# Counting matmuls of a routing search on four column quarters of the TensorE array

## The chip, the cores and the metric

The kernel runs on 1 core of one Trainium2 chip. The metric is device time in microseconds (us) of one execution, as the median of the runs shown. The profile is one further execution of the same program, with its own time.

## The reference, cut to what matters

Three layers follow each other: a retention attention (8 batches, 8 heads, 576 positions, head size 64), a mixture of 8 experts of which every token uses one, and a dense two-layer block. What the change touches is how tokens are given to experts:

```python
logits = x @ w_gate                      # x: 4608 tokens x 512, 8 experts
order = np.argsort(-logits.flatten())
for idx in order:                        # greedy: the highest logits first
    tok, e = idx // E, idx % E
    if assigned[tok] >= 0 or counts[e] >= cap:      # cap = N // E = 576
        continue
    assigned[tok] = e
    counts[e] += 1
for e in range(E):
    out[assigned == e] = np.maximum(x[assigned == e] @ w1[e], 0) @ w2[e]
...
h = x @ w_in                             # 4608 x 512 @ 512 x 2048
return (np.maximum(h, 0) + alpha * np.minimum(h, 0)) @ w_out
```

## The kernel before

**Stages.** First the attention is worked through in 36 chunks of 128 tokens; it leaves the rows in DRAM and the logits `Lg` (128 partitions x 36 chunks x 8 experts) on chip. Then a loop over `k` from 0 to 7 takes one expert at a time: `expert(k, ...)` runs that expert's two layers on its 576 tokens (matmul lines L913 and L932 to L934), and `second(...)` runs the dense block on 512 of them (first layer L969 to L971, second layer L960 and L991). A last call of `second` does the 64 tokens that are left of each expert. The f32 numbers are split in a high and a low part, so every product takes three matmuls.

**The routing.** `route(k)` finds which expert fills up k-th and which tokens are its own. `route(0)` runs by itself between attention and the first expert. `route(k + 1)` for the others is a generator that runs beside the work on expert `k`: at each call of `tick()` inside `expert` and `second` it writes its next few instructions into the same queues and stops at its next `yield`. A tick in `expert` or the first layer of `second` stands after 12 or 24 matmuls. Nothing reorders the queues afterwards: what stands in an engine's queue runs in that order. Routings 1 to 6 are the same; routing 7 only takes what is left.

**A search in six steps.** A routing looks for the value at which some expert is full. It tries 64, 32, 32, 32, 32 and 65 thresholds in its six steps (`STEPS`). In each step:

- VectorE compares the keys with all thresholds, into `G` (128 x 36 chunks x thresholds, bf16), in two halves of 18 chunks (`compare`, L427).
- One or two ticks later TensorE counts: for each chunk, the 8 columns of `O` (which token has which expert as its best) are the stationary operand and the chunk's part of `G` streams through. The counts add up in a PSUM tile `misc`, 8 rows (experts) by thresholds. Steps 0 and 5 use `counts` (L433): 36 matmuls of 64 or 65 columns with 8 columns of weights, all on the same columns of the array. Steps 1 to 4 use `counts2` (L438): 18 matmuls, each for two chunks, 64 columns long with 40 columns of weights (`O2` holds one chunk's 8 columns at 0 and the next chunk's at 32).
- At the next tick VectorE compares the counts with the room that each expert has (`ind`). After `counts2` it first subtracts the second chunk's counts from the room (`left`, L518) and compares with the first's (L519); after `counts` one instruction (L521) does it.
- At the tick after that TensorE spreads `ind` over 128 partitions (L524), and at the next VectorE adds it up (`sj`, L528), from which the next step's thresholds follow.

`O2` is filled by two ScalarE copies (L457) in the tick in which VectorE has made `O` (L399 to L403). The next tick makes the keys (L405 to L412), the one after it the first comparison.

**What stands around it in the queues.** In `expert`, each matmul tile is taken out of PSUM by ScalarE (L918) and then VectorE (L919, which also reads what L918 wrote). In `second`, VectorE (L974, L976), ScalarE (L978) and VectorE (L979) make `hl` from the first layer's tile. Weights that are new are split by ScalarE (L798) and VectorE (L799); the dense block's weights are split once, during expert 0, and read back split afterwards.

Of the kernel before, what the change touches and what calls it, by code (L numbers as in the profile page):

```python
# [10 lines left out]
F32 = mybir.dt.float32  # L11
F32R = mybir.dt.float32r
BF = mybir.dt.bfloat16
# [4 lines left out]
AF = mybir.ActivationFunctionType  # L18
OP = mybir.AluOpType
# [5 lines left out]
NCH = 36  # L25
# [70 lines left out]
def fused_kernel(ctx: ExitStack, tc: tile.TileContext, att: bass.AP, tab: bass.AP, wg: bass.AP,  # L96
                 w12: bass.AP, w34: bass.AP, alpha: bass.AP, out: bass.AP):
    nc = tc.nc
    V, P, ACT, PE = nc.vector, nc.gpsimd, nc.scalar, nc.tensor
# [3 lines left out]
    keep = ctx.enter_context(tc.tile_pool(name="keep", bufs=1))  # L103
    rt = ctx.enter_context(tc.tile_pool(name="route", bufs=1))
    pr = ctx.enter_context(tc.tile_pool(name="pr", bufs=1, space=bass.MemoryType.PSUM))
# [233 lines left out]


    O = keep.tile([128, NCH, 8], BF, name="O")
    O2 = keep.tile([128, NCH // 2, 40], BF, name="O2")
    vm = keep.tile([128, NCH], F32, name="vm")
    hf = keep.tile([128, NCH], F32, name="hf")
    lf = keep.tile([128, NCH], F32, name="lf")
# [2 lines left out]
    R8 = keep.tile([8, 1], F32, name="R8")  # L348
# [8 lines left out]
    def route_consts():  # L357
        V.tensor_copy(RT[:, 36:38], CONST["pcol"])
        C2["j01"] = CONST["j01"].rearrange("p (z j) -> p z j", z=2)
        V.memset(O2, 0.0)  # L360
        V.memset(Aw, 0.0)
        V.memset(tsum, 0.0)
        V.memset(R8, float(CAP))
        V.memset(ones8, 1.0)
        V.memset(ones8f, 1.0)
        V.tensor_copy(tri, CONST["tri"])
        V.tensor_copy(trii, CONST["trii"])
# [20 lines left out]
    def jt(s):  # L388
        return CONST["jtab"][:, JOFF[s]:JOFF[s + 1]]
# [31 lines left out]
    GT = {}  # L421
# [10 lines left out]
        for c in range(a, b):  # L432
            PE.matmul(GT["p"][0:8, :w], O[:, c, :], GT["G"][:, c, :w], start=c == 0, stop=c == NCH - 1)  # L433

    def counts2(w):

        for i in range(NCH // 2):
            PE.matmul(GT["p"][0:40, :2 * w].rearrange("p (a b) -> p a b", a=2), O2[:, i, :],  # L438
                      GT["G"][:, 2 * i:2 * i + 2, :w], start=i == 0, stop=i == NCH // 2 - 1)

    EXP, IDX, GI = {}, {}, {}

    def route(k):

        ecol, wcol = CONST["ecol"], CONST["wcol"]
        if k == 7:
            m = small("m")
            V.tensor_reduce(m, Lg, axis=AX.X, op=OP.max)
            t8 = small("t8", 1)
            V.tensor_scalar(t8, tsum, -1.0, 36.0, op0=OP.mult, op1=OP.add)  # L450
        else:
            if k:
                best, high, low = prep(0, NCH)
                emit(best)
                Oz = O.rearrange("p (i z) e -> p z i e", z=2)
                for z in range(2):
                    ACT.activation(O2[:, :, 32 * z:32 * z + 8], Oz[:, z], AF.Copy)  # L457
                yield
                emit(high, low)
                yield  # L460
            key, thr, n = hf, jt(0), None
            u = []
            for s, (z, w) in enumerate(STEPS):
                if s == 3:

                    Hb = small("Hb", 1)
                    V.scalar_tensor_tensor(Hb, n, 1.0, u[1], op0=OP.mult, op1=OP.add)
                    key = small("key")
                    V.tensor_scalar(key, hf, Hb, 131072.0, op0=OP.subtract, op1=OP.mult)
                    V.tensor_tensor(key, key, lf, op=OP.add)  # L470
                    thr = jt(3)
                elif s:
                    th = small("thr", 65)
                    V.scalar_tensor_tensor(th[:, :w], n.to_broadcast([128, w]), float(STEPS[s - 1][0]), tb,
                                           op0=OP.mult, op1=OP.add)
                    thr = th[:, :w]
                if k or s:
                    cuts = CUTS if not k else (0, 18, 36)
                    for a, b in zip(cuts, cuts[1:]):
                        compare(key, thr, w, a, b)  # L480
                    if k:
                        yield
                        if s == 5:
                            yield
                    if k and w == 32:
                        counts2(w)
                    else:
                        for a, b in zip(cuts, cuts[1:]):
                            counts(w, a, b)
                else:  # L490
                    best, high, low = prep(33, 36)
                    best.pop(0)()
                    emit(high, best)
                    compare(key, thr, w, 33, 36)
                    emit(low)
                    counts(w, 33, 36)

                if s in (1, 4):
                    tbt = small("tb", 65)
                    V.scalar_tensor_tensor(tbt[:, :STEPS[s + 1][1]], n.to_broadcast([128, STEPS[s + 1][1]]),  # L500
                                           float(STEPS[s - 1][0]), jt(s + 1), op0=OP.mult, op1=OP.add)
                    tb = tbt[:, :STEPS[s + 1][1]]
                    ua = small("ua", 1)
                    zz = STEPS[s - 1][0] + STEPS[s][0] + STEPS[s + 1][0]
                    V.tensor_scalar(ua, n, float(STEPS[s - 1][0]), float((-32768 if s == 1 else 0) - zz),
                                    op0=OP.mult, op1=OP.add)
                elif s in (0, 3):
                    tb = jt(s + 1)
                else:
                    ub = small("ub", 1)  # L510
                    V.scalar_tensor_tensor(ub, n, float(STEPS[s - 1][0]), ua, op0=OP.mult, op1=OP.add)
                    u = [ua, ub]
                yield
                p = GT["p"]
                ind = rt.tile([8, 65], BF, name="ind")
                if k and w == 32:
                    left = rt.tile([8, 32], F32, name="left")
                    V.tensor_scalar(left, p[32:40, w:2 * w], -1.0, R8[:, 0:1], op0=OP.mult, op1=OP.add)  # L518
                    V.tensor_tensor(ind[:, :w], p[0:8, :w], left, op=OP.is_ge)  # L519
                else:  # L520
                    V.tensor_scalar(ind[:, :w], p[0:8, :w], R8[:, 0:1], None, op0=OP.is_ge)  # L521
                if k:
                    yield
                PE.matmul(p[:, 128:128 + w], ones8, ind[:, :w], start=True, stop=True)  # L524
                yield
                sj = small("sj", 65)
                n = small("n", 1, bufs=2)
                V.tensor_scalar(sj[:, :w], p[:, 128:128 + w], 0.5, 0.0, op0=OP.is_ge, op1=OP.add, accum_out=n)  # L528

            j01 = C2["j01"]  # L530
            s8 = rt.tile([8, 2], F32, name="s8")
            cc = rt.tile([8, 2], F32, name="cc")
            for zi in range(2):
                scr = rt.tile([8, 65], F32, name="scr", bufs=2)
                V.scalar_tensor_tensor(scr, j01[0:8, zi, :], n[0:8, :], p[0:8, 0:65], op0=OP.is_equal,
                                       op1=OP.mult, accum_out=cc[:, zi:zi + 1])
            V.tensor_tensor(s8[:, 0:1], cc[:, 0:1], R8, op=OP.is_ge)
            V.tensor_tensor(s8[:, 1:2], R8, cc[:, 1:2], op=OP.subtract)
            D = rt.tile([8, 2, 8], F32, name="D")
            V.tensor_tensor(D, ident[0:8, None, 0:8].to_broadcast([8, 2, 8]),  # L540
                            s8.unsqueeze(2).to_broadcast([8, 2, 8]), op=OP.mult)
            if k:
                yield
            PE.matmul(p[:, 256:272], ones8f, D.rearrange("p a b -> p (a b)"), start=True, stop=True)
            T = small("T", 1)
            V.scalar_tensor_tensor(T, n, 1.0, u[1], op0=OP.mult, op1=OP.add)
            gt = small("gt")
            V.tensor_scalar(gt, key, T, None, op0=OP.is_gt)
            e01 = small("e01")
            V.tensor_scalar(e01, key, T, None, op0=OP.is_equal)  # L550
            gv_ = small("gv_")
            V.tensor_tensor(gv_, gt, vm, op=OP.mult)
            V.tensor_tensor(Aw, Aw, gv_, op=OP.add)
            yield
            zc = small("zc", 8)
            V.scalar_tensor_tensor(zc, p[:, 256:264], -100.0, ecol, op0=OP.mult, op1=OP.add)
            zm = small("zm", 1)
            V.tensor_reduce(zm, zc, axis=AX.X, op=OP.min)
            t8 = small("t8", 1)
            V.tensor_scalar(t8, zm, -1.0, -92.0, op0=OP.mult, op1=OP.add)  # L560
            nd = small("nd", 8)
            need = small("need", 1)
            V.scalar_tensor_tensor(nd, zc, zm, p[:, 264:272], op0=OP.is_equal, op1=OP.mult, accum_out=need)
# [557 lines left out]
```

## Time and profile before

| | |
|---|---|
| time, median of 3 runs | 1522.86 us (1520.42 to 1523.47) |
| the profiled execution's own time | 1522.37 us |
| its span, first to last instruction | 1520.5 us |
| TensorE busy | 1459.2 us, 96% of the span |
| VectorE busy | 904.7 us, 59% |
| ScalarE busy | 397.0 us, 26% |
| mean granted TensorE clock | 0.983 of full speed |

The span is what the trace covers; the time adds 1.9 us before and after it. TensorE is busy almost throughout, so a VectorE or ScalarE instruction counts only where TensorE waits for it. Starts in the trace are measured; the ends of matmuls are modelled, so the pace of a series of matmuls is read from the start of its first to the start of what follows.

### The profile page before, as it was taken

To read this page: it belongs to the slowest core of one execution; us is meant where nothing else is said; L and a number is where in the kernel's file an instruction comes from. 1 tells how busy PE (TensorE), PEld (TensorE's weight loads), DVE (VectorE), ACT (ScalarE), POOL (GpSimd) and SP (SyncE) were. 2 spreads that over 40 slices of the span, in tenths; PEclk is the share of its full clock that TensorE was granted. 3 is DMA by queue.
4 is the path that set the end of the run, shared out by engine and by line. 5 is a ranking of instruction groups with operands and counts; after the bars stand their busy time and mean duration, and the time that the engine had idled before them with its cause. 6 is when DMAs were issued, how large, how long until landed. Compare 5 with 4: busy or idle time off the path is not lost.

```text
span 1520.5 us, 24973 instructions
## 1 busy us (share of the span) xinstructions
PE 1459.2 (96%) x10124; PEld 1275.1 (84%) x10124; DVE 904.7 (59%) x2013; ACT 397.0 (26%) x752; POOL 179.0 (12%) x195
## 2 busy tenths in 40 slices
PE   9899948999899999999999999999999999999997
PEld 8888848978797889788978897889789888988886
DVE  4878877477745674667456745674566434333433
ACT  4566613222421132114101410141014212311111
POOL 3455501001100110011001100110012001000101
PEclk9999968999999999999999999999999999999999
DMA  8999814369634743474347444734575565345652
GB/s 306 350 341 341 306 64 142 125 251 286 197 112 166 236 138 132 150 238 132 139 166 218 129 139 168 223 124 141 187 215 165 158 233 179 108 167 193 221 194 83
DMA packets 97938, 287.50 MB, mean 189 GB/s; under 512 B 45984, under 2 KB 46368, under 8 KB 79392
## 3 DMA queue, kind: packets, MB, share of 16 engines
q1 hardware_dynamic: 78400, 230.12, 45.6%
q10 hardware_dynamic: 13344, 35.87, 6.2%
q0 software_dynamic: 6080, 19.93, 3.9%
q8 instruction: 79, 1.29, 0.3%
q14 instruction: 35, 0.29, 0.1%
HBM read 232.67 MB, written 44.04 MB: 182 GB/s over the span
## 4 chain that ended last, share of the span: by engine, by line
PE 60%; issue 16%; DVE 12%; ACT 7%; DMA 2%; POOL 1%; SPq 1%; ACTq 1%; POOLq 0%
PE acc L960 15%; PE mm L969 6%; PE mm L971 6%; PE mm L970 6%; PE mm L913 4%; PE acc L913 4%; DVE whl L799 2%; PE mm L932 2%; PE acc L932 2%; PE acc L933 2%; PE mm L933 2%; PE acc L934 2%; PE mm L934 2%; DVE cv_r L226 2%; ACT whl L798 2%
## 5 line engine op out<-in xcount | busy, mean ns | idle before, releaser
L960 PE MATMUL acc<-whl,hl 128*128 128x512 f32 x1608 | 388.2, 391 | 0.0
L960 PEld LDWEIGHTS acc<-whl,hl 128*128 128x128 f32 x1608 | 299.9, 188 | 62.5 <-ACT hl L978 0.4
L978 ACT ACTIVATE hl<-tmp 128x512 fp32r<-128x512 f32 x144 | 91.0, 632 | 651.2 <-DVE tmp L976 651.2
L974 DVE TENSOR_SCALAR tmp<-mm,AL 128x512 f32<-128x512 f32 x144 | 107.7, 748 | 200.7 <-PE mm L971 200.1
L969 PE MATMUL mm<-act,whl 128*128 128x512 f32 x512 | 203.3, 397 | 3.9 <-ACT whl L798 2.4
L971 PE MATMUL mm<-act,whl 128*128 128x512 f32 x512 | 200.0, 391 | 0.0
L970 PE MATMUL mm<-act,whl 128*128 128x512 f32 x512 | 199.9, 390 | 0.0
L979 DVE TENSOR_TENSOR hl<-tmp,hl 128x512 fp32r<-128x512 f32 x144 | 99.7, 692 | 110.5 <-ACT hl L978 110.5
L824 POOL DMA_INDIRECT rows<-x_rows,gi x40 | 42.4, 1060 | 706.0 <-DVE ec L638 533.1
L969 PEld LDWEIGHTS mm<-act,whl 128*128 128x128 f32 x512 | 96.5, 188 | 24.8 <-ACT whl L798 2.8
L971 PEld LDWEIGHTS mm<-act,whl 128*128 128x128 f32 x512 | 96.3, 188 | 21.0 <-DVE whl L799 0.8
L799 DVE TENSOR_TENSOR whl<-raw,whl 128x1024 fp32r<-128x1024 f32 x80 | 97.7, 1223 | 25.5 <-ACT whl L798 25.2
L970 PEld LDWEIGHTS mm<-act,whl 128*128 128x128 f32 x512 | 96.6, 189 | 19.0
L913 PE MATMUL mm<-act,whl 128*128 128x288 f32 (+2 forms) x768 | 109.5, 299 | 0.7 <-ACT act L854 0.7
L913 PE MATMUL acc<-act,whl 128*128 128x288 f32 (+2 forms) x768 | 108.0, 298 | 0.0
L913 PEld LDWEIGHTS mm<-act,whl 128*128 128x128 f32 x768 | 105.7, 192 | 2.1 <-ACT act L854 1.1
L913 PEld LDWEIGHTS acc<-act,whl 128*128 128x128 f32 x768 | 104.4, 190 | 0.3
L976 DVE SCALAR_TENSOR_TENSOR tmp<-mm,tmp 128x512 f32<-128x512 f32 x144 | 99.6, 692 | 5.0
L798 ACT ACTIVATE whl<-raw 128x1024 fp32r<-128x1024 f32 x80 | 84.1, 1052 | 26.3 <-DVE gi L646 26.3
L1003 POOL DMA_INDIRECT out<-rows,ix x32 | 34.9, 1091 | 444.8 <-DVE rows L999 439.6
L932 PE MATMUL mm<-act,whl 128*128 128x288 f32 x256 | 76.8, 300 | 0.0
L932 PE MATMUL acc<-act,whl 128*128 128x288 f32 x256 | 76.6, 299 | 0.0
(233 smaller groups left out, 2240.5 us busy)
## 6 DMA issues: line engine op xcount, KB each, us to landing
whl<-w_parts SPq DMA_DIRECT2D x128, 1024.0 KB, 4.8
raw<-in_w SPq DMA_DIRECT2D x64, 512.0 KB, 4.4
a_in<-in_att SPq DMA_DIRECT2D x34, 768.0 KB, 6.8
cv_in<-in_w SPq DMA_DIRECT2D x32, 512.0 KB, 7.8
w_parts<-whl ACTq DMA_DIRECT2D x16, 1024.0 KB, 6.3
x_rows<-xn ACTq DMA_DIRECT2D x36, 256.0 KB, 5.4
w_f<-cv_r ACTq DMA_DIRECT2D x32, 256.0 KB, 6.9
raw<-w_f SPq DMA_DIRECT2D x16, 512.0 KB, 5.8
```

The source lines that it names most:

```text
L798: ACT.activation(w[:, 0], t, AF.Copy)
L799: V.tensor_tensor(w[:, 1], t, w[:, 0].bitcast(F32), op=OP.subtract)
L913: PE.matmul(ps, w[:, wi, wc], x[:, xi, c, hh], start=(wi, xi, c) == (0, 0, 0), stop=(xi, c) == (1, 3))
L932: PE.matmul(ps, w[:, 0, cs], h[:, 0, c % 4, hh], start=c == 0, stop=False)
L960: PE.matmul(acc[tt], hl[:, hi, tt * 128:tt * 128 + 128], w[:, wi, 512:1024], start=f == 0 and (wi, hi) == (0, 0), stop=False)
L969: PE.matmul(ps, w[:, 0, cs], y[:, 0, c, 0:512], start=c == 0, stop=False)
L970: PE.matmul(ps, w[:, 0, cs], y[:, 1, c, 0:512], start=False, stop=False)
L971: PE.matmul(ps, w[:, 1, cs], y[:, 0, c, 0:512], start=False, stop=c == 3)
L974: V.tensor_scalar(t, ps, 0.0, AL[:, f:f + 1], op0=OP.min, op1=OP.mult)
L976: V.scalar_tensor_tensor(g, ps, 0.0, t, op0=OP.max, op1=OP.add)
L978: ACT.activation(hl[:, 0], g, AF.Copy)
L979: V.tensor_tensor(hl[:, 1], g, hl[:, 0].bitcast(F32), op=OP.subtract)
```

## The change

From routing 1 on, `counts` and `counts2` give way to `counts4` in all six steps. It issues one matmul for each chunk, with the 8 columns of `O` as weights; chunk `c` goes to column quarter `c % 4` of the array and so to rows 0, 32, 64 or 96 of the PSUM tile. VectorE then adds the four groups of rows into `tot` and compares that. `O2`, its two ScalarE copies and `left` are gone. Routing 0 keeps `counts`.

```diff
-    def counts2(w):
-
-        for i in range(NCH // 2):
-            PE.matmul(GT["p"][0:40, :2 * w].rearrange("p (a b) -> p a b", a=2), O2[:, i, :],
-                      GT["G"][:, 2 * i:2 * i + 2, :w], start=i == 0, stop=i == NCH // 2 - 1)
+    def counts4(w):
+
+        GT["p"] = pr.tile([128, 512], F32, name="misc")
+        for c in range(NCH):
+            r = 32 * (c % 4)
+            PE.matmul(GT["p"][r:r + 8, :w], O[:, c, :], GT["G"][:, c, :w], start=c < 4, stop=c >= NCH - 4,
+                      tile_position=(0, r))
...
                 emit(best)
-                Oz = O.rearrange("p (i z) e -> p z i e", z=2)
-                for z in range(2):
-                    ACT.activation(O2[:, :, 32 * z:32 * z + 8], Oz[:, z], AF.Copy)
                 yield
...
-                    if k and w == 32:
-                        counts2(w)
+                    if k:
+                        counts4(w)
                     else:
                         for a, b in zip(cuts, cuts[1:]):
                             counts(w, a, b)
...
-                if k and w == 32:
-                    left = rt.tile([8, 32], F32, name="left")
-                    V.tensor_scalar(left, p[32:40, w:2 * w], -1.0, R8[:, 0:1], op0=OP.mult, op1=OP.add)
-                    V.tensor_tensor(ind[:, :w], p[0:8, :w], left, op=OP.is_ge)
-                else:
-                    V.tensor_scalar(ind[:, :w], p[0:8, :w], R8[:, 0:1], None, op0=OP.is_ge)
+                tot = p[0:8, 0:65]
+                if k:
+
+                    tot = rt.tile([8, 65], F32, name="tot")
+                    V.tensor_copy(tot[:, :w], p[32:40, :w])
+                    V.tensor_tensor(tot[:, :w], p[64:72, :w], tot[:, :w], op=OP.add)
+                    V.tensor_tensor(tot[:, :w], p[96:104, :w], tot[:, :w], op=OP.add)
+                    V.tensor_tensor(tot[:, :w], p[0:8, :w], tot[:, :w], op=OP.add)
+                V.tensor_scalar(ind[:, :w], tot[:, :w], R8[:, 0:1], None, op0=OP.is_ge)
```

On ScalarE, at the place in routing 3 where `O` has just been made (during expert 2), the queue before read as follows.

```order
L798 ACTIVATE whl<-raw 128x1024
L918 ACTIVATE act<-mm 128x288
L457 ACTIVATE O_127<-O 128x18x8 x2
L918 ACTIVATE act<-mm 128x288 x2
L918 ACTIVATE act<-acc_6293 128x288
L798 ACTIVATE whl<-raw 128x1024
```

The two L457 copies, which wait for VectorE's `O`, stood ahead of the next PSUM evictions; in the changed program they are gone and the six rows are the same without them.

On VectorE, between the counting and the spreading of step 0 in routing 2, the queue before held one instruction, L521.

```order
L919 SCALAR_TENSOR_TENSOR act<-mm,act 128x288
L521 TENSOR_SCALAR ind<-misc,R_133 8x64
L919 SCALAR_TENSOR_TENSOR act<-mm,act 128x288
L919 SCALAR_TENSOR_TENSOR act<-acc_4978,act 128x288
```

The changed program holds five there, one behind the other (line numbers of the changed file).

```order
L919 SCALAR_TENSOR_TENSOR act<-mm,act 128x288
L517 COPY tot<-misc 8x64
L518 TENSOR_TENSOR tot<-misc,tot 8x64
L519 TENSOR_TENSOR tot<-misc,tot 8x64
L520 TENSOR_TENSOR tot<-misc,tot 8x64
L521 TENSOR_SCALAR ind<-tot,R_132 8x64
L919 SCALAR_TENSOR_TENSOR act<-mm,act 128x288
L919 SCALAR_TENSOR_TENSOR act<-acc_5075,act 128x288
```

The place among the evictions L919 is the same; in steps 1 to 4 the five take the place of two (L518 and L519 of before). No tick and no DMA has moved.

## Rows read from the trace of the kernel before

**Rows 1.** The page: busy time, share of span, instructions.

```profile
PE 1459.2 (96%) x10124; PEld 1275.1 (84%) x10124; DVE 904.7 (59%) x2013; ACT 397.0 (26%) x752; POOL 179.0 (12%) x195
```

**Rows 2.** Timeline of PE, a counting of step 1 (start, us, engine, line, [idle before]).

```profile
427.62 0.73 PE L438 MATMUL misc<-G,O 128*40 128x64 bf16 x18
428.28 0.40 PE L932 MATMUL mm<-act,whl 128*128 128x288 f32 x1
```

**Rows 3.** Timeline of PE, a counting of step 5.

```profile
323.14 1.32 PE L433 MATMUL misc<-G,O 128*8 128x65 bf16 x36
324.39 0.96 PE L960 MATMUL acc<-whl,hl 128*128 128x512 f32 x3
```

**Rows 4.** Timeline of all engines, from `O` to step 0's counting in routing 3.

```profile
555.92 0.54 ACT L457 ACTIVATE O<-O 128x144 bf16<-128x144 bf16 x2 [3.68 <-DVE O L403]
...
556.78 0.82 DVE L919 SCALAR_TENSOR_TENSOR act<-mm,act 128x288 fp32r<-128x288 f32 x2 [0.90 <-ACT act L918]
...
559.27 0.41 ACT L918 ACTIVATE act<-acc 128x288 fp32r<-128x288 f32 x1 [0.38 <-PE acc L913]
559.99 0.45 DVE L919 SCALAR_TENSOR_TENSOR act<-acc,act 128x288 fp32r<-128x288 f32 x1
...
561.76 0.72 PE L433 MATMUL misc<-G,O 128*8 128x64 bf16 x18 [0.93 <-DVE G L427]
...
563.03 0.72 PE L433 MATMUL misc<-G,O 128*8 128x64 bf16 x18 [0.54 <-DVE G L427]
...
563.68 1.58 PE L913 MATMUL mm<-act,whl 128*128 128x288 f32 x10
```

**Rows 5.** Timeline, the same place in routing 1.

```profile
257.42 0.49 DVE L919 SCALAR_TENSOR_TENSOR act<-acc,act 128x320 fp32r<-128x320 f32 x1 [0.93 <-ACT act L918]
...
262.07 0.72 PE L433 MATMUL misc<-G,O 128*8 128x64 bf16 x18 [2.08 <-DVE G L427]
```

**Rows 6.** Timeline of PE in the attention: matmuls on halves of the array.

```profile
75.67 1.05 PE L284 MATMUL oT<-a_in,sblk 128*128 128x128 f32 x8
76.65 1.09 PE L288 MATMUL oT<-pt,vs 128*64 128x128 f32 x16
77.58 0.64 PE L308 MATMUL S<-vs,a_in 128*64 128x64 f32 x16
...
78.69 0.27 PE L260 MATMUL pA<-a_in,kt 64*128 64x128 f32 x1
78.70 0.27 PE L261 MATMUL pB<-a_in,kt 64*128 64x128 f32 x1
78.80 0.27 PE L260 MATMUL pA<-a_in,kt 64*128 64x128 f32 x1
```

**Rows 7.** Timeline of PE, the shortest matmuls at the full clock.

```profile
350.44 0.29 PE L606 MATMUL misc<-RT,W 128*128 128x38 f16 x5
350.58 0.47 PE L969 MATMUL mm<-act,whl 128*128 128x512 f32 x1
```

**Rows 8.** Groups by form: VectorE on counts (busy us, mean ns | idle before).

```profile
L518 DVE TENSOR_SCALAR left<-misc,R 8x32 f32<-8x32 f32 x24 | 5.8, 242 | 1.1 <-PE misc L438 0.4
L519 DVE TENSOR_TENSOR ind<-misc,left 8x32 bf16<-8x32 f32 x24 | 4.3, 179 | 0.8
```

**Rows 9.** Timeline, `ind` and its reader on PE, routing 2, step 4.

```profile
470.75 0.18 DVE L519 TENSOR_TENSOR ind<-misc,left 8x32 bf16<-8x32 f32 x1
...
473.81 0.18 PE L524 MATMUL misc<-ind,ones 8*128 8x32 bf16 x1
```

**Rows 10.** Timeline, VectorE and PE beside routing 1, late in expert 0.

```profile
330.17 0.75 DVE L974 TENSOR_SCALAR tmp<-mm,AL 128x512 f32<-128x512 f32 x1 [0.44 <-PE mm L971]
...
383.43 0.79 PE L969 MATMUL mm<-act,whl 128*128 128x512 f32 x1 [2.39 <-ACT whl L798]
```

**Rows 11.** Stretches: busy by engine, granted clock (PEclk), DMA share.

```profile
264.00:267.40 3.40, 3.40 (x17) 3.40 (x16) 2.08 (x6) 0.38 (x1) 0.00 (x0) 0.50 0.23 52
...
559.00:564.00 5.00, 3.53 (x52) 3.13 (x51) 5.00 (x8) 1.77 (x3) 0.00 (x0) 1.00 0.35 105
```

More of the change, by code (lines that the diff above doesn't have):

```diff
@@ L341, in fused_kernel @@
     O = keep.tile([128, NCH, 8], BF, name="O")
-    O2 = keep.tile([128, NCH // 2, 40], BF, name="O2")
     vm = keep.tile([128, NCH], F32, name="vm")
@@ L359, in route_consts @@
         C2["j01"] = CONST["j01"].rearrange("p (z j) -> p z j", z=2)
-        V.memset(O2, 0.0)
         V.memset(Aw, 0.0)
@@ L534, in route @@
                 scr = rt.tile([8, 65], F32, name="scr", bufs=2)
-                V.scalar_tensor_tensor(scr, j01[0:8, zi, :], n[0:8, :], p[0:8, 0:65], op0=OP.is_equal,
+                V.scalar_tensor_tensor(scr, j01[0:8, zi, :], n[0:8, :], tot, op0=OP.is_equal,
                                        op1=OP.mult, accum_out=cc[:, zi:zi + 1])
```

## The prediction, made before the changed kernel was run

> **What bounds the kernel now.** I read the page first: TensorE is busy for 96% of the span [rows 1]. From the first expert on, what TensorE does and what it waits for is the time, and the other engines count where it waits for them. So I went to the timeline of TensorE at the counting matmuls, to see what one counting costs and whether TensorE waits ahead of it, and then to VectorE and ScalarE at the few places where it does.
>
> A counting of steps 1 to 4 takes 0.66 us from its first matmul to the next expert matmul [rows 2]; no wait stands ahead of it. About 0.12 us of that is the way from the last counting matmul back to the f32 matmuls; I come to it by taking the 36 equal matmuls of rows 3 at 31 ns, and it stays in every version. So 18 matmuls of 64 columns go at 30 ns each. A counting of step 5 takes 1.25 us [rows 3]. Step 0 is different: in routing 3 TensorE waits 0.93 us for the first half of G and 0.54 us for the second, and the second half's matmuls take 0.65 us [rows 4]. Routings 4 to 6 look the same; routing 1 waits 2.08 us ahead of its first half [rows 5]; routing 2 does not wait.
>
> **The pace of four quarters.** This decides nearly everything, and the trace of before does not show it. What it shows is halves. Sixteen f32 matmuls that alternate between two column halves take 0.93 us, 58 ns each, where eight of the same length on the whole array take 0.98 us, 0.12 us each [rows 6]. Two on the two row halves start 0.01 us apart, and the next pair 0.11 us after the first [rows 6]. So tiles of the array do run at the same time, weight loads included, and a pair costs what one costs. On one tile the shortest matmuls seen, 38 columns, come every 28 ns [rows 7], hardly faster than 64 columns at 30 ns.
>
> If four quarters work as two halves do, a round of four costs what one matmul of that length costs on its tile: 28 ns for 32 columns, 30 ns for 64. Four starts 7 ns apart (the pair's distance, which two digits show as 0.00 to 0.01) fill the same 28 ns. So 7.5 ns for each matmul, nine rounds in 0.27 us. The other end is that matmuls of any tile come no faster than the shortest seen, 26 to 28 ns each. I take 7.5 ns, since the pairs, with their starts 0.01 us apart, speak against a limit on starts.
>
> **The change part by part**, for routings 2 to 6 first.
>
> - Steps 1 to 4, 20 countings: 18 matmuls become 36, 0.27 + 0.12 = 0.39 us for 0.66, so -0.27 each, -5.4 us.
> - Step 5, 5 countings: 0.39 for 1.25 us, -0.86 each, -4.3 us.
> - Step 0 of routing 2: the same, about -0.8 us.
> - Step 0 of routings 3 to 6: the first half's 18 matmuls only wait longer for the second half of G. Behind that, 18 x 7.5 ns + 0.12 = 0.26 us take the place of 0.65, -0.39 each, -1.6 us.
> - The two ScalarE copies of O. They hold ScalarE for 3.68 us until VectorE has made O, with evictions queued behind, and VectorE then idles 0.90 us for one of these [rows 4]. Without them VectorE goes straight on, but not by the whole 0.90: its L919 at 559.99 reads what ScalarE's L918 wrote, which waited for TensorE and ended at 559.68 [rows 4]. So G comes 0.3 us sooner, and TensorE waits that much less: 4 x -0.3 = -1.2 us. In routing 2 there is no wait to shorten.
> - VectorE's sums. An add on 8 rows costs about what L519 costs, 179 ns, and I take that for the copy too; the comparison, an instruction of L518's kind, 242 ns [rows 8]. So steps 1 to 4 take 4 x 0.18 + 0.24 = 0.96 us for 0.42, +0.54; steps 0 and 5 gain four instructions on somewhat wider rows, +0.85. Their reader is L524, a tick later. In step 4 of routing 2 it starts 2.9 us after ind is made [rows 9], about the least that I found in routings 2 to 6. So this costs nothing there. Were the slack gone, each routing would pay 4 x 0.54 + 2 x 0.85 = 3.9 us.
>
> That is -13.3 us for routings 2 to 6.
>
> Routing 1 runs beside expert 0, where the dense block's weights are split for the first time. There VectorE falls behind: in the stretch up to 383 us it has hardly a gap, the last wait for TensorE being 0.44 us at 330.17, and TensorE in the end waits 2.39 us for weights that come out of this chain [rows 10]. Up to about 302 us TensorE leads: step 0 gives 0.93 (VectorE's idle time behind the copies, [rows 5], nothing else being late there) + 0.39, steps 1 to 3 0.27 each, so -2.1 us. After that VectorE's extra sums of steps 4 and 5 go on its chain, +0.54 and +0.85, and TensorE's gains there are lost in the waits. Net -0.7 us; ends 0 and -3.
>
> The sum is -14.0 us against the profiled execution's 1522.37, 1508.4. The median of the runs lies 0.5 us higher than that execution; I say 1509.
>
> **The rivals.**
>
> *A limit on starts: slower.* Each counting matmul costs 26 ns wherever it goes. The five step 5 countings give only 1.25 - (36 x 0.026 + 0.12) = 0.19 us each, -1.0; the step 0 ones -0.2 in routing 2 and 4 x -0.36 with the 0.3 us of the copies, -1.6 together; but the 20 short countings take 1.06 for 0.66 us, +8.0. Routing 1 adds about +1. Together +6.4, 1529. For it: nothing in the trace comes faster on the average than 28 ns, since the halves too have two matmuls in 58 ns or more. Against it: the starts within a pair. The change breaks even at about 20 ns for a matmul.
>
> The Trainium skill, TensorEngine Tiling (Array Packing), "Instruction Overhead", says that a small dimension should not be the one that pays for tiling, since a matmul has some 60 cycles of overhead. TensorE: Matmul & The Clock Gate, "Wait — 56ns, not 53.3ns?", states a floor of 25 ns between starts, and its "The mechanism" states starts 4 ns apart on different tiles. By the floor the time would be this rival's, by the second the forecast's; rows 7 agree with the floor on one tile and rows 6 with the near starts on two, and no row here has four.
>
> *Two at a time.* The trace shows pairs only; if two quarters run together and not four, a matmul costs 14 to 15 ns. The short countings gain nothing (0.64 for 0.66), step 5 gives 0.6 us each, step 0 about 2.8 in all: -6, 1516.5.
>
> *The clock.* After routing 1's waits the granted clock is 0.50, the lower of its two levels (1.2 GHz), for 3.4 us [rows 11]; around routing 3's shorter ones it stays at 1.00 [rows 11]. With quick counting matmuls the idle time of step 0 gets longer in sum (0.63 + 0.93 us where 0.93 + 0.54 stood). If the clock falls in routings 3 to 6, 3.4 us at half speed cost 1.7 us each, so 1515; if it no longer falls in routing 1, it gives 1.7 us back.
>
> *VectorE's sums reach TensorE* after all: 6 x 3.9 = 23 us at most on top of the forecast, 1531. It decides only from 2.9 us of delay on; against it stands the slack.
>
> **How the numbers follow.** Forecast 0.54; two at a time or another pace in between 0.14; the clock 0.06; paces near 20 ns, which end within 0.2% (3 us, about what a measurement of this kernel can tell), 0.08; a limit on starts 0.16; VectorE 0.02. So faster 0.74, same 0.08, slower 0.18. The forecast's own range is 1504 (routing 1 keeps its gains, the clock stays up) to 1513 (10 ns). For 8 in 10 it reaches over two at a time to the paces near 20 ns: 1504 to 1522.
>
> **What would show it.** Right: counting matmuls of the four quarters in rounds of about 30 ns, 0.4 us from a counting's first matmul to the next expert matmul in steps 1 to 5; the wait ahead of step 0 in routings 3 to 6 at 0.6 us for 0.93; no wait of L524 for ind in routings 2 to 6. Wrong: countings of 1.0 us, granted clock 0.50 after a step 0 of routings 3 to 6, or L524 waiting for VectorE.

## Result and the profile after

The changed kernel takes 1499.82 us (median of 4 runs, 1498.49 to 1502.52) where the kernel before, run beside it, took 1521.99 (1520.42 to 1523.47): ratio 0.9859, interval 0.9845 to 0.9874, some 22 us faster. The forecast was 1509.0, its range 1504 to 1522, so the time lies 4 us below the range: the direction was right, the gain was 1.6 times the forecast.

The profiled execution took 1498.49 us. Its page still shows a TensorE that is busy for 96% of the span, now with 21.6 us less of work than in [rows 1]:

```profile
PE 1437.6 (96%) x10556; PEld 1255.3 (84%) x10556; DVE 926.5 (62%) x2132; ACT 396.4 (26%) x740; POOL 179.4 (12%) x195
```

The timeline of TensorE at a counting of step 1, one of step 5 (both routing 2), and step 0 of routing 3; the bracket is the idle time ahead:

```profile
420.85 0.41 PE L438 MATMUL misc<-G,O 128*8 128x32 bf16 x36
421.19 0.40 PE L932 MATMUL mm<-act,whl 128*128 128x288 f32 x1
...
474.26 0.45 PE L438 MATMUL misc<-G,O 128*8 128x65 bf16 x36
474.65 0.50 PE L969 MATMUL mm<-act,whl 128*128 128x512 f32 x1
...
551.85 0.32 PE L438 MATMUL misc<-G,O 128*8 128x64 bf16 x18
553.09 0.32 PE L438 MATMUL misc<-G,O 128*8 128x64 bf16 x18 [0.93 <-DVE G L425]
553.34 1.85 PE L913 MATMUL mm<-act,whl 128*128 128x288 f32 x12
```

The first pair answers to [rows 2]: 0.34 us from the first counting matmul to the next expert matmul, where 0.66 stood. The second answers to [rows 3]: 0.39 for 1.25. The last three answer to [rows 4]: the wait of 0.93 us ahead of the first half of G is gone, all of it; the one ahead of the second half grew from 0.54 to 0.93, as the first half's matmuls no longer fill that time; and the second half takes 0.25 us for 0.65.

The timelines of VectorE and ScalarE ahead of that counting:

```profile
546.85 0.81 DVE L919 SCALAR_TENSOR_TENSOR act<-mm,act 128x288 fp32r<-128x288 f32 x2
547.18 0.41 ACT L918 ACTIVATE act<-acc 128x288 fp32r<-128x288 f32 x1 [0.23 <-PE acc L913]
...
548.76 0.41 ACT L918 ACTIVATE act<-acc 128x288 fp32r<-128x288 f32 x1 [1.17 <-PE acc L913]
550.05 0.45 DVE L919 SCALAR_TENSOR_TENSOR act<-acc,act 128x288 fp32r<-128x288 f32 x1
550.36 0.41 ACT L918 ACTIVATE act<-acc 128x288 fp32r<-128x288 f32 x1 [1.18 <-PE acc L913]
550.42 2.62 DVE L425 TENSOR_TENSOR G<-hf,tables 128x1152 bf16<-128x1152 f32 x2
```

VectorE has no idle time left here. Its L919 at 550.05, the last instruction ahead of the comparison, begins before ScalarE's L918 at 550.36; so it can't read what that L918 writes, as the prediction had it of the same two instructions in [rows 4]. The program issues one L918 and then one L919 for each tile, so the two pair off by count (128 of each in the trace): the L919 at 550.05 is the 37th, and the 37th L918 is the one at 547.18, two further back. In the kernel before, by the same count, the L919 at 559.99 reads the first of these two, which ended at 558.60:

```profile
558.18 0.72 ACT L918 ACTIVATE act<-acc 128x288 fp32r<-128x288 f32 x2
```

TensorE's waits from 240 to 1130 us by what ended them (us in all, times, longest):

```profile
PE misc L438 <- DVE G L425: 6.0, 7, 1.1
...
PE misc L524 <- DVE ind L521: 2.2, 1, 2.2
PE acc L991 <- ACT hl L978: 1.0, 1, 1.0
```

VectorE's sums reach TensorE once in the whole run, and the rows of VectorE and TensorE there show where: step 5 of routing 1, in expert 0.

```profile
325.29 0.22 DVE L517 COPY tot<-misc 8x65 f32<-8x65 f32 x1
...
326.31 0.25 DVE L521 TENSOR_SCALAR ind<-tot,R 8x65 bf16<-8x65 f32 x1
...
326.61 0.18 PE L524 MATMUL misc<-ind,ones 8*128 8x65 bf16 x1 [2.16 <-DVE ind L521]
```

Where the time went, by the starts of the same matmuls in both profiled executions (after less before, us):

| stretch | measured | forecast |
|---|---|---|
| up to 241 us (before), ahead of routing 1's first counting | -2.6 | 0 |
| from there to the start of expert 1 (400.18 before, 394.41 after) | -3.2 | -0.7 |
| expert 1 to the end, routings 2 to 6 | -18.0 | -13.3 |
| sum | -23.8 | -14.0 |

In each of routings 3 to 6, step 0 gives -1.0 (the wait) and -0.42 (the second half), steps 1 to 4 -0.32 each, step 5 -0.87; 0.25 more goes near L991 at two places (694 and 1142 us before). The forecast had -0.3, -0.39, -0.27 and -0.86.

The first 2.6 us lie ahead of the first counting that the change touches, and are no work of the change. Half of them, 1.3 us, come in the attention, where TensorE's waits at L322 were shorter in this execution, most of it at one place (the kernel before, then the changed one):

```profile
132.86 1.17 PE L322 MATMUL px<-xw,xT 128*128 128x136 f32 x8 [1.45 <-DVE xT L291]
...
131.56 1.17 PE L322 MATMUL px<-xw,xT 128*128 128x136 f32 x8 [0.45 <-DVE xT L291]
```

The other half comes between 228 and 241 us, with the clock. The stretch table of the kernel before, then of the changed one (busy time by engine, granted clock, DMA share, GB/s), around 202 to 242 us, and at expert 0's end, with one row of the changed kernel inside routing 1's step 0:

```profile
202.00:242.00 40.00, 21.33 (x257) 19.12 (x258) 31.11 (x131) 5.39 (x10) 5.38 (x5) 0.53 0.31 102
395.60:400.20 4.60, 4.56 (x13) 3.30 (x14) 4.32 (x8) 2.37 (x4) 0.00 (x0) 0.66 0.81 263
```

```profile
202.00:242.00 40.00, 22.38 (x280) 20.51 (x280) 31.51 (x124) 6.04 (x10) 6.03 (x5) 0.62 0.37 121
...
391.20:394.50 3.30, 3.22 (x13) 2.37 (x14) 2.98 (x5) 1.50 (x3) 0.00 (x0) 1.00 0.99 365
...
261.00:264.20 3.20, 3.20 (x15) 3.20 (x15) 2.70 (x8) 0.38 (x1) 0.00 (x0) 0.50 0.41 118
```

In the first stretch TensorE was granted 0.53 of full speed before and 0.62 after; the lower level (0.50, 1.2 GHz) lasted 37.5 us from 202.56 in the one; in the other it lasted 27.3 us from 202.79 and came back for 3.4 us at 233.51. The profiles of the experiments show both lengths (37.5 in e1, e4, e6 and f1; 27.3, with 3.4 or 6.8 us more soon behind it, in e2, e3, e5, e7, e8 and e9), so it goes with the execution and not with the change. I count the whole 2.6 us out. By medians the change is worth 22 us, by the profiled pair without this 21.3. At expert 0's end the clock was at 0.50 for 3.4 us before and at 1.00 after: -1.4 us. That is one execution of each.

### The profile page after: what moved, and what is told of

It reads as the page before. It is cut to its first block, busy times and chain, and to the rows that moved or that the text cites. A ratio compares the mean times of both kernels' runs of the same rounds, so it can differ in the third digit from the quotient of the medians.

```text
span 1496.7 us, 25946 instructions
## 1 busy us (share of the span) xinstructions
PE 1437.6 (96%) x10556; PEld 1255.3 (84%) x10556; DVE 926.5 (62%) x2132; ACT 396.4 (26%) x740; POOL 179.4 (12%) x195
## 4 chain that ended last, share of the span: by engine, by line
PE 59%; issue 17%; DVE 13%; ACT 7%; DMA 2%; POOL 1%; ACTq 1%; SPq 0%; POOLq 0%
PE acc L960 15%; PE mm L969 6%; PE mm L971 6%; PE mm L970 6%; PE mm L913 4%; PE acc L913 4%; DVE whl L799 3%; PE mm L932 2%; PE acc L932 2%; PE mm L934 2%; PE acc L934 2%; PE acc L933 2%; PE mm L933 2%; ACT whl L798 2%; DVE cv_r L226 2%
## 5 line engine op out<-in xcount | busy, mean ns | idle before, releaser
L824 POOL DMA_INDIRECT rows<-x_rows,gi x40 | 43.1, 1077 | 684.8 <-DVE ec L638 514.6
L971 PEld LDWEIGHTS mm<-act,whl 128*128 128x128 f32 x512 | 96.5, 188 | 21.3 <-DVE whl L799 1.0
```

Source lines behind the costliest of these rows:

```text
L971: PE.matmul(ps, w[:, 1, cs], y[:, 0, c, 0:512], start=False, stop=c == 3)
```

## Experiments

Theory: (a) four quarters work at the same time, so a round of four costs what one matmul costs on its tile; (b) ScalarE's copies cost VectorE their whole idle time at step 0, and the granted clock beside it, which the forecast priced at a third; (c) VectorE's sums are hidden except in routing 1. Rivals: in each place the other way round, as the expectations say. Every kernel's time stands as a ratio to the kernel before, run beside it.

**e1: the change with the two copies back.** Nothing reads O2.

```diff
                 emit(best)
+                Oz = O.rearrange("p (i z) e -> p z i e", z=2)
+                for z in range(2):
+                    ACT.activation(O2[:, :, 32 * z:32 * z + 8], Oz[:, z], AF.Copy)
                 yield
```

> The changed kernel with the two ScalarE copies of O put back (into a tile that nothing reads). Theory: what the prediction missed is that, without the copies, VectorE goes on the whole 0.9 us earlier, because its eviction ahead of G reads an earlier ScalarE eviction than I had paired it with; so the first wait of step 0 comes back at 0.9 to 1.0 us in routings 1 and 3 to 6, and the time is 5 us above the changed kernel's 1499.8, about 1505. Rival: the copies are worth the 0.3 us in four routings that the prediction gave them, the wait comes back at 0.3 us, and the time is about 1501.

Measured: 1508.42 us, ratio 0.9918 (0.9904 to 0.9932). So the quarters and the sums by themselves give -12.5 us (-14.6 to -10.3), and the copies take 8.6 us back. VectorE and TensorE in routing 3 (L923, L439 and L426 are L919, L438 and L425 of the changed kernel), then the stretch behind:

```profile
552.56 0.82 DVE L923 SCALAR_TENSOR_TENSOR act<-mm,act 128x288 fp32r<-128x288 f32 x2 [0.90 <-ACT O L458]
...
557.53 0.32 PE L439 MATMUL misc<-G,O 128*8 128x64 bf16 x18 [0.92 <-DVE G L426]
558.80 0.32 PE L439 MATMUL misc<-G,O 128*8 128x64 bf16 x18 [0.95 <-DVE G L426]
```

```profile
559.90:563.20 3.30, 3.30 (x16) 3.30 (x15) 2.04 (x5) 0.41 (x1) 0.00 (x0) 0.50 0.02 5
```

VectorE's idle 0.90 us is back, and so is the whole first wait. Behind the two waits, of 0.92 and 0.95 us within 2.2 us, the granted clock is at 0.50 for 3.4 us in this routing (+1.5 us), which neither parent shows at this place; at expert 0's end a wait of L991 that is 1.1 us longer and a second such stretch cost 2.5 together, and a stretch at 380 us that the changed kernel has is missing, -0.8. With five waits of 1.0 to 1.1 this makes the 8.7 us that the profiles differ by behind the first counting. The waits are theory (b), and more than I had put on it. The clock is less regular: in routings 4 to 6 of the same execution the same two waits stand, and the clock stays at 1.00. Routing 4, waits and stretch:

```profile
705.86 0.32 PE L439 MATMUL misc<-G,O 128*8 128x64 bf16 x18 [0.93 <-DVE G L426]
707.13 0.32 PE L439 MATMUL misc<-G,O 128*8 128x64 bf16 x18 [0.95 <-DVE G L426]
...
705.00:712.00 7.00, 5.19 (x71) 4.99 (x72) 6.24 (x13) 2.15 (x4) 0.00 (x0) 1.00 0.23 78
```

**f1: the kernel before, with its copies on GpSimd.**

```diff
-                    ACT.activation(O2[:, :, 32 * z:32 * z + 8], Oz[:, z], AF.Copy)
+                    P.tensor_copy(O2[:, :, 32 * z:32 * z + 8], Oz[:, z])
```

> The kernel before, with the two copies of O into O2 on GpSimd instead of ScalarE and nothing else changed. Theory: what the copies cost is ScalarE's wait for O with PSUM evictions queued behind it, so this alone takes away the first wait of step 0 in routings 3 to 6 (0.93 us each) and about 0.9 of routing 1's 2.08: -4.6 us against before, 1516. Rival: the gain of the changed kernel at step 0 comes from its short countings or from other timing, and the copies' place is worth 0.3 us in four routings: 1520.

Measured: 1514.29 us, ratio 0.9949 (0.9936 to 0.9963), -7.2 us (-9.7 to -5.6). The profiled execution took 1519.83 us, the longest of its runs: up to 240 us, ahead of the first counting, it had lost 4.2 us on the kernel before (a low stretch of the clock at 76 us and an earlier start of the long one among them); from there on it is 6.8 us faster. GpSimd, VectorE and TensorE in routing 3:

```profile
557.44 0.55 POOL L457 COPY O<-O 128x144 bf16<-128x144 bf16 x2 [3.75 <-PE acc L913]
557.23 0.81 DVE L919 SCALAR_TENSOR_TENSOR act<-mm,act 128x288 fp32r<-128x288 f32 x2
...
562.20 0.72 PE L433 MATMUL misc<-G,O 128*8 128x64 bf16 x18
563.47 0.72 PE L433 MATMUL misc<-G,O 128*8 128x64 bf16 x18 [0.54 <-DVE G L427]
```

The copies are still made; they only no longer stand in ScalarE's queue ahead of the evictions. VectorE's idle time and TensorE's first wait go, -0.9 us in routings 3 to 6 and -1.0 in routing 1, and at expert 0's end L991's wait is 1.2 us for 1.9 and the low stretch of the clock is missing as well. This settles that it was the queue, and not the quarters, that made the first wait.

**e2, e3, e4: how many quarters, and in which order.** e2 sends all 36 matmuls to one quarter, without sums; e3 uses two, with two instructions of sums fewer; e4 gives each quarter nine chunks in turn.

```diff
-            r = 32 * (c % 4)
+            r = 0                  (e2; start and stop at the first and last chunk)
+            r = 32 * (c % 2)       (e3)
+            r = 32 * (c // 9)      (e4)
```

> The changed kernel with all 36 counting matmuls of each step on one column quarter and without VectorE's sums: the 32-wide matmuls on one tile at the full clock. Theory: a tile takes no matmul faster than about 26 ns, so a short counting takes 36 x 0.026 + 0.12 = 1.05 us for 0.34, 24 times +0.7, step 5 goes back to 1.25 us for 0.38 (6 times +0.87), step 0 +0.85 once and +0.4 five times: about +25 us, 1524. Rival: 32 columns go at half the time of 64 also on one tile (15 ns), so that four quarters gave only a factor of two: a short counting 0.66 us, +0.32 each, in all about +16, 1515.

> The changed kernel with chunks on two column quarters (0 and 32) and two groups of rows to add. Theory: the pace is a tile's own 26 to 30 ns divided by the number of tiles, so 13 ns for 32 columns and 15 for 64: a short counting 0.58 us for 0.34, +0.24 in 24, step 5 +0.28 in 6, step 0 about +1.0 in all: +8.5, 1508. Rival: starts come every 6.6 ns whatever the number of tiles is (two or more), so the time stays at 1500.

> The changed kernel with the same four quarters and sums, but chunks 0 to 8 on the first, 9 to 17 on the second and so on, so that a matmul's neighbour in the queue is on the same tile. Theory: matmuls start in the order of the queue, so each waits for the one before it on its tile and nothing overlaps but at three borders: as on one quarter, about 1.0 us for a short counting, about +24 us, 1524. Rival: TensorE takes matmuls of another tile ahead of waiting ones, and the pace stays near 7 ns: 1500.

Measured: e2 1519.77 us, ratio 0.9996 (0.9984 to 1.0007); e3 1505.98, 0.9905 (0.9891 to 0.9920); e4 1514.25, 0.9958 (0.9944 to 0.9973). One counting of step 1 in routing 2 on TensorE's timeline in e2, in e3 and in e4:

```profile
420.78 1.06 PE L438 MATMUL misc<-G,O 128*8 128x32 bf16 x36
```

```profile
421.32 0.61 PE L438 MATMUL misc<-G,O 128*8 128x32 bf16 x36
```

```profile
424.91 0.79 PE L438 MATMUL misc<-G,O 128*8 128x32 bf16 x36
```

The distances between starts in these bursts, as the trace records them (ns, the first twelve of 35, and all 35 together):

```
one quarter      29 25 25 25 25 25 25 25 25 25 26 25 ...   884
two, in turn      3 25  4 21  4 21  4 21  5 20  5 20 ...   438
four, in turn     3  3  4 18  3  4  3 15  3  5  3 14 ...   231
four, in blocks  28 25 25 25 25  6 19 10 15 10 16  9 ...   608
```

A matmul of 32 columns comes every 25 ns on one quarter, and a round of two or of four takes those same 25 ns. With 65 columns it is 32 ns on one quarter, and a round of four takes 30. That is theory (a), at 6.6 ns for a matmul where the forecast had 7.5. e2's time lies between the theory's and the rival's: its 24 short countings are 0.33 us longer than before's paired ones (1.21 us from the matmul ahead to the one behind, for 0.875), +8.0, and the removal of the copies gives 7.2 back (f1). Against its theory (1524) it lacks the sums, and so the wait of 2.16 us, and the low stretches that the changed kernel has at 261 and 380 us. e3 lies nearer its theory (1508) than its rival (1500), and its pace of 12.5 ns decides between them. e4 came out between its theory (1524) and its rival (1500): mean distance 17 ns, not 25 and not 6.6. Its distances read as two series of 25 ns laid over one another at each border between blocks, for about four matmuls; in the rest of a block the distances stay at 25 ns. Records don't name the quarter, so this reading is not shown, and how TensorE came to start a new block's matmuls there stays open. The order in turn is in any case the better one by 14 us.

The Trainium skill, TensorE: Matmul & The Clock Gate, "The mechanism", has starts about 4 ns apart on different tiles, and the 3 to 5 ns inside a round agree. The floor of 25 ns between starts that the same page's "Wait — 56ns, not 53.3ns?" gives is what e2 shows, for one tile: it did not bind four.

**e6: four more adds in each step's sums.** The changed kernel, with four extra instructions between L520 and L521 whose result nothing reads.

```diff
+                    for r in (32, 64, 96, 0):
+                        V.tensor_tensor(more[:, :w], p[r:r + 8, :w], tot[:, :w], op=OP.add)
```

> The changed kernel with four more VectorE additions in every step (into a tile that nothing reads), so that the sums cost about 0.75 to 0.9 us more a step. Theory: in routings 2 to 6 the reader of the counts has 1.9 us and more to spare, so no new wait of L524 shows there; in routing 1 VectorE is behind, and step 5's wait of L524 (2.2 us) grows by 1 to 2 us, half of which is taken back at the end of expert 0: 1501 to 1502. Rival: the sums hold up what is queued behind them, and TensorE pays a good part of 6 x 5 us: above 1510.

Measured: 1506.54 us (1503.66 to 1511.21), ratio 0.9906 (0.9884 to 0.9928). Neither number was met, but the trace says which part is which. TensorE's only wait for the sums in e3 (two instructions of them), then its two in e6 (eight):

```profile
326.94 0.18 PE L522 MATMUL misc<-ind,ones 8*128 8x65 bf16 x1 [1.03 <-DVE ind L519]
```

```profile
313.79 0.17 PE L528 MATMUL misc<-ind,ones 8*128 8x32 bf16 x1 [0.41 <-DVE ind L525]
...
332.03 0.18 PE L528 MATMUL misc<-ind,ones 8*128 8x65 bf16 x1 [3.05 <-DVE ind L525]
```

No wait in e2 without sums, 1.03 us with two, 2.16 with four (above), 3.05 with eight, always at step 5 of routing 1; with eight a second wait of 0.41 us shows at step 4 of the same routing. These places pay for VectorE's time; in the later routings no add shows. From the start of expert 1 to the end, e6 stays 7.5 to 8.0 us behind the changed kernel: 120 added instructions in routings 2 to 6 cost 0.5 us at most. Of the 7.5, 3.7 lie ahead of the first counting (1.0 in the attention, most of the rest with the longer low stretch of the clock), 0.8 come from step 4's wait and one of L964 behind it, 0.9 are the longer wait, and 1.6 a stretch of clock 0.50 from 332.87 that follows it. So the later routings bear out theory (c). How much of the medians' 6.7 us is the clock is not shown: one execution of e6 was profiled, and all four lie above those of the changed kernel.

**e5 and e7: step 0 counted a tick later.** To take away the second wait of step 0 (0.93 us), e5 lets a tick pass between the comparison and the counting; e7 also folds the comparison of steps 1 to 4 into the sums, one VectorE instruction fewer.

```diff
-                        if s == 5:
+                        if s in (0, 5):
                             yield
```

> The changed kernel with one tick more between step 0's comparison and its counting. Theory: what is left of step 0's wait (0.93 us for the second half of G in routings 3 to 6, 2.0 in routing 1) is only that the counting stands too early in TensorE's queue, so it goes away: -5.8 us, 1494. Rival: the routing then ends a tick later, its rows are gathered later, and the next expert's first matmuls or the end of expert 0 wait for as much as is won: 1500.

> As the kernel with the later counting of step 0, and with the room subtracted in the first of VectorE's four instructions, so that the comparison takes the last addition's place in steps 0 to 4 (one instruction fewer). Theory: the saved 0.2 us a step counts only in routing 1, where VectorE is behind: 0.2 to 1 us less than the kernel with the later counting alone, 1493.5. Rival: no difference from it.

Measured: e5 1503.87 us, ratio 0.9888 (0.9872 to 0.9905); e7 1503.63, 0.9886 (0.9869 to 0.9903). Both 4 us slower than the changed kernel: a miss of 10. Step 0's wait did go in routings 3 to 6; others came. TensorE's timeline in e5 at the start of expert 2 and at routing 3's step 0, then its waits from 400 to 1130 us:

```profile
538.39 3.55 PE L913 MATMUL mm<-act,whl 128*128 128x288 f32 x24 [0.64 <-ACT act L874]
542.42 1.86 PE L913 MATMUL mm<-act,whl 128*128 128x288 f32 x12 [0.47 <-ACT act L874]
...
555.33 0.45 PE L438 MATMUL misc<-G,O 128*8 128x64 bf16 x36
```

```profile
PE mm L913 <- ACT act L874: 7.5, 10, 2.4
```

A routing that takes one tick more ends one tick later, and behind it in the same sequence of ticks stands the placing of the next expert's input. ScalarE's L874, which writes it, is now what the first matmuls of experts 2 to 6 wait for: 7.5 us in ten waits, against four waits of 0.93 saved. That is the rival's mechanism, at more than its price. e7 shows once more that VectorE's instruction count doesn't matter here.

**e8 and e9: the same tick given and another taken.** e8 makes the choice of experts and the halves of the scores in one tick instead of two, so that e5's extra tick leaves the routing's length as it was. e9 leaves the low halves for later still.

```diff
                 emit(best)
-                yield
                 emit(high, low)
                 yield
...
-                        if s == 5:
+                        if s in (0, 5):
```

> The change, with the tick that e5 puts between step 0's comparison and its counting taken out again ahead of it: VectorE makes the one-hot choice (L397 to L401) and the halves of the scores (L403 to L410) in one tick instead of two, so the routing ends in the same tick as in the change. Theory (e5 lost because the gathered rows came a tick later, 1.1 us of waits at each expert's first matmuls): the second wait of step 0 (0.93 us, 5 times) goes and nothing comes back, 1494 to 1496. Rival (VectorE, with 3.4 us of choice and halves in one tick, is late with L919 and TensorE waits there): 1500 or more.

> As e8, with the low halves (L409, L410, 0.36 us) made only behind step 0's comparison, which is the first step that does not need them. Theory: the same time as e8 within 1 us, since the tick has room. Rival (VectorE's room in the first tick decides): 1 to 2 us faster than e8.

Measured: e8 1495.03 us (1493.92 to 1497.5), ratio 0.9837 (0.9823 to 0.9852); e9 1495.26, 0.9843 (0.9827 to 0.9860). The theory's 1494 to 1496, and no difference between the two. One correction to the expectation's words: in e5 it was not the gather that was late (GpSimd's L824 starts at 503.90 us there and at 504.95 in the changed kernel) but the placing behind it. TensorE in e8, in routing 1 (two places) and at step 0 of routing 3:

```profile
264.97 0.18 PE L523 MATMUL misc<-ind,ones 8*128 8x64 bf16 x1 [2.04 <-DVE ind L520]
...
326.68 0.18 PE L523 MATMUL misc<-ind,ones 8*128 8x65 bf16 x1 [2.17 <-DVE ind L520]
...
551.42 0.45 PE L438 MATMUL misc<-G,O 128*8 128x64 bf16 x36
```

All 36 matmuls run in one piece, -1.1 us in each of routings 3 to 6. In routing 1, where VectorE is the slower one, the sums of step 0 now show as a wait of 2.04 us in place of those for G. e8 is the fastest version found, 4.8 us under the changed kernel by the medians, 4.6 by the profiles.

## Why the forecast fell short, step by step

- **The pace of four quarters** was right in its mechanism and nearly in its size: 6.6 ns for 7.5, 0.34 us for 0.39 in the short countings (-0.32 each for -0.27, the last matmul ahead of the burst counted in), -0.87 for -0.86 in step 5, -0.42 for -0.39 in step 0. The 28 ns that the prediction reads for one tile in [rows 7] is five matmuls with the start of what follows; their own starts lie 39, 26, 25 and 25 ns apart. The forecast's -14.0 is made of -2.1 for the copies (4 x 0.3, and 0.93 in routing 1) and -11.9 for all else; e1 measured all else at -12.5.
- **"L919 at 559.99 reads what ScalarE's L918 wrote, ... and ended at 559.68"** is the step that failed. This is the term of the copies, -0.3 us for each of routings 3 to 6. I paired two instructions because the one began soon after the other ended. The L918 that this L919 reads had ended at 558.60, so nothing held VectorE there, and it kept all of its 0.90 us, and TensorE 1.0 in each of routings 3 to 6 for the 0.3 forecast: -2.8 us. With what follows at expert 0's end (L991's wait and the low stretch) the copies are worth 7.2 us (f1) to 8.6 (e1) for 2.1; e1's sum holds the low stretch of routing 3, which came in one routing of four.
- **Routing 1** was forecast at -0.7, with ends 0 and -3, and came to -3.2. The chain was read rightly: VectorE is late there, and L524 does wait for the sums, 2.16 us. But I took TensorE's later waits to swallow the gains, and they shrank instead: L991's wait for ScalarE from 1.9 to 1.0 us, and the low stretch of the clock at 397 us is gone. With nothing but the copies' place changed (f1) the wait is 1.2 us and the stretch is missing; with the copies put back (e1) the wait is 2.1 and the stretch is there. The copies are not all that sets this wait, since e2 to e4, without them, wait 2.5 to 4.1 us at L991; and that the clock follows the wait is not shown, since e2 kept the full clock.
- **VectorE's sums** cost nothing in routings 2 to 6, as forecast; e6 bounds four more at 0.5 us.
- **The rivals.** A limit on starts and two at a time fall with e2 and e3. The clock did not fall in routings 3 to 6; it stayed at 0.50 for 3.4 us in routing 1 (the row at 261, as in [rows 11]). Where it changed, at expert 0's end, it gave 1.4 us back. The prediction had a term for the clock in routing 1's step 0 and none for that place.

What stays open: how long the low clock ahead of expert 0 lasts in a given execution, and with it some 3 us of any single profile; and what decides whether the clock falls behind waits of this size, since it fell in one of four alike in e1.

## What to carry over

Many small matmuls that accumulate are to be dealt out to the column quarters in turn, not in blocks, and then cost, here, a quarter of what they cost on one. A small instruction in an engine's queue is priced by what stands behind it: two copies of 0.32 us cost 7 to 9 us over routings 1 to 6. Before a wait is only partly credited because "the next input is late too", find the very instruction that wrote that input, by counting writers and readers, and not by which ended last.

## What the hardware showed that I had not expected

Matmuls of 32 columns on one 128 x 32 tile come every 25 ns (e2), as the 38-column ones of [rows 7] do behind their first 39 ns. The four quarters in turn start 3 to 5 ns apart and then wait for the round's 25 ns to pass, so four cost what one does even at this shortest length. And the granted clock fell to 0.50 for 3.4 us behind two waits of 0.92 and 0.95 us in routing 3 of e1, and stayed at 1.00 behind the same two waits in routings 4 to 6 of the same execution. At L991 it fell behind a wait of 1.94 us (the kernel before) and not behind one of 2.46 (e2). So in these traces the length of a wait does not tell by itself whether the clock falls.
